# Agent attention and two feed-forward layers: the first batch's softmax over keys with its maximum in two halves, values among the scores

## The chip, the cores and the metric

The kernel runs on one core of one Trainium2 chip. The metric is device time in microseconds (us), from three runs of the same program, and the profile is one further execution of it. A NeuronCore has a matrix engine (TensorE, PE in the profile; its loads of stationary operands are a row of their own, PEld), a vector engine (VectorE, DVE), a scalar engine (ScalarE, ACT), GpSimd (POOL) and SyncE (SP), which here starts the transfers from memory. The engines run side by side, each takes its own instructions in order, and they wait for each other through semaphores. TensorE's clock has two levels, 1.2 and 2.4 GHz; the profile tells which share of full speed was granted in a stretch.

## The reference

```python
def _attn_ref(q, k, v, agents):               # q, k, v: (2, 12480, 128), agents: (2, 49, 128)
    scale = 1.0 / np.sqrt(q.shape[-1])
    def sm(a, b):
        s = scale * (a @ b.transpose(0, 2, 1))
        s = s - s.max(-1, keepdims=True)
        e = np.exp(s)
        return e / (e.sum(-1, keepdims=True) + 1e-09)
    a2k = sm(agents, k)
    agent_v = a2k @ v
    return (sm(q, agents) @ agent_v).astype(np.float32)
# x = that, as (24960, 128); w_in (128, 2048) and w_out (2048, 128) of each layer
h = x @ w_in;  x = ((h * np.cos(h)) @ w_out).astype(np.float32)
h = np.maximum(x @ w_in2, 0.0);  out = (h * h @ w_out2).astype(np.float32)
```

The four weight matrices come as 64-bit floats, everything else as 32-bit floats.

## The kernel before

The work has three stretches.

**The prologue** (lines 405 to 507) handles the first batch's keys and values and has to end before the first block of queries can start. The keys come as 13 transfers of 960 keys (`k_load`), each worked on in two halves of 480. `k_scores` multiplies a half with the agents (four matmuls of 120 keys, each printed by the trace as two instructions, since the operands are 32-bit floats), copies the scores to `s_t` on ACT and keeps a running maximum `rm` on DVE. Although one batch is wanted here, its moving operand holds the agents of both batches: 98 columns (`both` is True, lines 284 to 288). After the last of the 26 halves the maximum is finished: `k_max` reduces `rm`, `k_max0` turns it on PE, `k_max1` takes the maximum over keys, `k_max2` spreads it to all partitions with a second small matmul. Then `k_shift` subtracts it and `exps` takes the exponential, in five parts (`parts`), and `v_mm` multiplies each of the 13 groups of 960 with their values into one PSUM bank, `pav` (8 matmuls, 16 instructions a group). `agent_v` divides, and a short chain (`agent_v1`, `agent_v2`, `m_fast`) makes the first columns of the matrix `ms` that the first layer needs.

While this runs, pieces of the weights are converted from 64-bit floats: there are 16 pieces of 512 columns, 0 to 3 for `w_in1`, 4 to 7 for `w_out1`, 8 to 11 for `w_in2`, 12 to 15 for `w_out2`. `scale` is one instruction on ACT and one on POOL, `stage` four on DVE, `high` one on ACT, `add` three matmuls on PE (from piece 4 on), `low` one on ACT. For pieces above 8 the `t` of the four stages lies in PSUM.

Tables say what is loaded and done after which half or group: `LOAD0`, `LOADK`, `LOADV` for transfers (k, v, w for a piece, q), `EVK`, `EVV` for the rest. Loads of keys and values share 7 buffers in rotation, so a transfer waits until the group that is 7 places ahead has been used.

**The fill**, the first 8 of 416 steps (`FILL`; 52 blocks of 480 queries, 8 steps each). A step `s` does `stage_a` (two 128-wide chunks of the first layer: `h1_chunk` on PE, the sine on ACT, the product `g` on DVE, its high half `gh`), `stage_b` of an earlier step (six matmuls into `px` with `gh` and the remainder `gl`), and after the fill `stage_c` and `stage_d` of the second layer as well. Small tasks are hung on steps with `at(step, slot, ...)`: the rest of the weight pieces (a loop over tuples: piece, step of its load, step `s0` of its `scale`; the stages come at `s0 + 1`, `high` at `s0 + 2`, `add` and `low` at `s0 + 4`), the columns of `ms`, the queries' softmax. When block 0's `px` is complete, in step 8's turn, ACT makes `xh` and DVE `xl` from it (lines 746 and 747), which `stage_c` of step 9 waits for.

**The steady stretch**, steps 9 to 415, in which the second batch's keys and values are worked in between.

All is under a manual schedule: each engine runs its instructions in the order in which the code issues them.

Of the kernel before, what the change touches and what calls it, by code (L numbers as in the profile page):

```python
# [34 lines left out]
def agent_attention_moe_kernel(ctx, tc, q, k, v, agents, w_in1, w_out1, w_in2, w_out2, out):  # L35
# [19 lines left out]
    NKV, NRAW = 7, 4  # L55
# [46 lines left out]
    class Weights:  # L102
# [20 lines left out]
        def stage(self, i):  # L123
# [3 lines left out]
            if i == 0:  # L127

                self.a = tmp(0, 4) if self.n == 2 * NWP else tmp(1, 4)

                self.t = pso.tile([128, 512], F32, name="t", tag="o")[:, :WP] if self.n > 2 * NWP else None
# [52 lines left out]

    def stages(ws):
        for i in range(Weights.STAGES):
            for w in ws:
                w.stage(i)
# [93 lines left out]
    def k_scores(b, n, kT, ps, both):  # L282

        w = B * A if both else A
        for j in range(J):
            o = ps[:TP, j * w:(j + 1) * w]
            rhs = agT.rearrange("p b a -> p (b a)") if both else agT[:, b, :]
            nc.tensor.matmul(o, kT[:, j * TP:(j + 1) * TP], rhs, start=True, stop=True)
        sv = ps[:TP, :J * w].rearrange("p (t a) -> p t a", a=w)[:, :, b * A if both else 0:][:, :, :A]
        sn = s_t[:, n * J:(n + 1) * J, :]  # L290
        nc.scalar.activation(sn, sv, AF.Copy)
        h = n % 2
        eng = nc.vector
        if n // 2 == 1:
            eng.tensor_tensor(rm[:, h], s_t[:, h * J:(h + 1) * J, :], sn, ALU.max)
        elif n > 1:
            eng.tensor_tensor(rm[:, h], rm[:, h], sn, ALU.max)
# [10 lines left out]

    def k_max1(pm):
        ma = ag.tile([A, 1], F32, name="ma")  # L310
        nc.vector.tensor_reduce(ma, pm[:A, :TP], axis=AX.X, op=ALU.max)
# [12 lines left out]
    cuts = [0] + [min(KCH * c, NT) for c in (1, 4, 7, 10)] + [NT]  # L324
    parts = [slice(a, b) for a, b in zip(cuts, cuts[1:]) if b > a]
# [5 lines left out]
    def k_exp(x):  # L331
        exps(s_t[:, parts[x], :])
# [55 lines left out]
    def out_copy(po):  # L388
# [6 lines left out]
    LOAD0 = "kkwwkkkkkww"  # L395
    LOADK = {1: "k", 3: "k", 5: "k", 7: "k", 9: "k", 11: "kqq", 13: "v", 15: "v", 17: "wv", 19: "wv", 21: "v",
             23: "wv", 25: "wv"}
    EVK = {3: ["y0"], 5: ["s0", "a0"], 11: ["t0", "y2"], 13: ["s2", "a2"]}
    LOADV = {0: "v", 1: "v", 2: "v", 3: "v", 4: "v", 5: "vw"}
    EVV = {0: ["k2", "y4", "k3", "q0", "s4"], 1: ["e0", "y6", "k4", "h4", "s6", "h6", "n0"], 8: ["z8", "u8"], 10: ["b8"]}  # L400
    EVK = {n: [(e[0], int(e[1:])) for e in x] for n, x in EVK.items()}
    EVV = {n: [(e[0], int(e[1:])) for e in x] for n, x in EVV.items()}
    with tc.manual_schedule():

        with ExitStack() as c1:
# [4 lines left out]
            kcs, qTs, vcs, ws = [], [], [], []  # L410

            def load_w():
                ws.append(Weights(len(ws), *((sp, "raw", NRAW) if 4 <= len(ws) < 8 else (ag, "ld", 4))))

            def load_kv():
                if len(kcs) < NKC:
                    kcs.append(k_load(0, len(kcs), sp, "kv", NKV))
                elif len(vcs) < NKC:
                    vcs.append(v_load(0, len(vcs), sp, "kv", NKV))

            def load_q():
                if len(qTs) < G0:
                    qTs.append(q_load(*blocks[len(qTs)], sp, G0))

            loads = {"k": load_kv, "v": load_kv, "w": load_w, "q": load_q}

            def load(what):
                for c in what:
                    loads[c]()

            def scale(m):
                for w in ws[m:m + 2]:
                    w.scale()

            def high(m):
                for w in ws[m:m + 2]:
                    w.high()

            def add(m):
                for w in ws[m:m + 2]:  # L440
                    w.add()

            def top(m):
                for w in ws[m:m + 2]:
                    w.top()

            def wtop(m):
                nc.vector.tensor_reduce(wmax[:, NWP:], wmax[:, :NWP], axis=AX.X, op=ALU.max)

            load(LOAD0)  # L450
            make_identity(nc, ident)
            nc.vector.tensor_copy(identr, ident)
            nc.vector.tensor_scalar(nidentr, ident, -1.0, None, ALU.mult)

            for n in range(2 * NKC):
                i, hf = divmod(n, 2)
                pool, tag = (ps1, "h1") if hf == 0 else (ps2, "h2")
                k_scores(0, n, kcs[i][:, hf * J * TP:(hf + 1) * J * TP], pool.tile([128, 512], F32, name="pks", tag=tag),
                         True)
                load(LOADK.get(n, ""))  # L460
                for f, m in EVK.get(n, ()):
                    {"y": scale, "s": lambda m: stages(ws[m:m + 2]), "a": add, "t": top}[f](m)
            mb = k_max2(k_max1(k_max0(k_max())))
            qs = []
            for n in range(G0):
                qs.append(Queries(q_products(blocks[n][0], qTs[n], ps1.tile([128, 512], F32, name="pq", tag="h1")),
                                  sg_of(n)))

            def k_part(x):
                k_shift(mb, parts[x])  # L470
                k_exp(x)

            def q_part(m):
                for x in qs:
                    x.scores()

            def q_exp(m):
                for x in qs:
                    exps(x.sg)

            k_part(0)
            k_part(1)
            top(2)
            wtop(0)
            pav = pso.tile([128, 512], F32, name="pav", tag="o")
            pts = {}

            def first_p(m):
                pts[0] = q_finish(xs[0])
                sines()  # L490

            for i in range(NKC):
                v_mm(pav, vcs[i], i, i == 0, i == NKC - 1)
                load(LOADV.get(i, ""))
                for f, m in EVV.get(i, ()):
                    {"y": scale, "s": lambda m: stages(ws[m:m + 2]), "h": high,
                     "z": lambda m: ws[m].scale(), "u": lambda m: stages(ws[m:m + 1]), "b": lambda m: ws[m].high(),
                     "k": k_part, "q": q_part, "e": q_exp,
                     "n": lambda m: qs[0].normalize(xs[0])}[f](m)
            av = agent_v(pav[:A, :C + 1])  # L500
            first_p(0)
# [29 lines left out]
        for n, s_load, s0 in ((5, None, -4), (6, None, -3), (7, None, -2), (8, None, -1), (9, -3, 0), (12, -3, 1), (13, -3, 2),  # L531
                              (10, -1, 3), (14, 2, 4), (11, 3, 5), (15, 4, 6)):
# [373 lines left out]
```

## Time and profile before

| what | us |
|---|---|
| median of three runs | 2214.27 (2213.15 to 2214.34) |
| the profiled execution: its own time, its span | 2214.8, 2213.0 |
| busy in the span: PE, DVE, ACT, POOL | 2188.5, 1936.4, 1516.6, 1280.7 |
| first scores matmul, last one done | 5.00, 30.15 |
| first values matmul, last one done | 36.24, 61.41 |
| first matmul of step 0 | 64.70 |
| first matmul of step 9 | 108.05 |

The span runs from the first to the last instruction; the profiled execution's own time is 1.8 us more, and it lies 0.5 us above the median. PE is busy for 99% of the span, but a busy PE is not a PE at its peak: instructions overlap, and the clock is not told by the busy time. DMA engines are busy in the first 60 us and little after that.

### The profile page before, as it was taken

To read this page: it belongs to the slowest core of one execution; us is meant where nothing else is said; L and a number is where in the kernel's file an instruction comes from. 1 tells how busy PE (TensorE), PEld (TensorE's weight loads), DVE (VectorE), ACT (ScalarE), POOL (GpSimd) and SP (SyncE) were. 2 spreads that over 40 slices of the span, in tenths; PEclk is the share of its full clock that TensorE was granted. 3 is DMA by queue.
4 is the path that set the end of the run, shared out by engine and by line. 5 is a ranking of instruction groups with operands and counts; after the bars stand their busy time and mean duration, and the time that the engine had idled before them with its cause. 6 is when DMAs were issued, how large, how long until landed. Compare 5 with 4: busy or idle time off the path is not lost.

```text
span 2213.0 us, 30063 instructions
## 1 busy us (share of the span) xinstructions
PE 2188.5 (99%) x10593; PEld 1876.3 (85%) x10593; DVE 1936.4 (88%) x2431; ACT 1516.6 (69%) x2453; POOL 1280.7 (58%) x1285
## 2 busy tenths in 40 slices
PE   8999999999999999999999999999999999999998
PEld 8688888888888888888888888888888888888886
DVE  7788888888899999999988888888988988888897
ACT  4666766667767767767667767767776776776764
POOL 1455555556556556656556656566566565655664
PEclk9999999999999999999999999999999999999999
DMA  9200010000010010010000000000000000000000
GB/s 343 87 27 19 28 45 28 19 19 18 19 36 19 19 36 19 19 42 22 10 17 11 10 19 10 11 17 10 19 10 10 19 10 19 10 9 15 5 10 11
DMA packets 24952, 62.08 MB, mean 28 GB/s; under 512 B 2883, under 2 KB 16195, under 8 KB 24795
## 3 DMA queue, kind: packets, MB, share of 16 engines
q1 hardware_dynamic: 24795, 60.10, 8.5%
q8 instruction: 85, 1.39, 0.3%
q14 instruction: 72, 0.59, 0.1%
HBM read 47.31 MB, written 12.78 MB: 27 GB/s over the span
## 4 chain that ended last, share of the span: by engine, by line
PE 90%; DVE 7%; issue 1%; ACT 1%; DMA 0%; POOL 0%; SPq 0%; POOLq 0%; ACTq 0%; DVEq 0%
PE po L386 8%; PE ph L379 8%; PE po L384 8%; PE px L384 8%; PE ph L386 8%; PE ph L385 8%; PE ph L384 8%; PE px L386 7%; PE po L385 7%; PE ph L380 7%; PE px L385 7%; DVE g L713 2%; DVE sl L782 2%; PE misc L198 2%; PE pav L336 1%
## 5 line engine op out<-in xcount | busy, mean ns | idle before, releaser
L717 POOL TENSOR_SCALAR gh<-g 128x480 fp32r<-128x480 f32 x824 | 796.1, 984 | 671.6 <-DVE g L713 528.8
L757 ACT ACTIVATE r<-ph 128x480 f32<-128x480 f32 x832 | 472.8, 572 | 518.2 <-PE ph L386 487.1
L731 DVE TENSOR_TENSOR gl<-g,gh 128x960 fp32r<-128x960 f32 x409 | 587.0, 1435 | 84.4 <-POOL gh L717 84.3
L776 POOL TENSOR_SCALAR sh<-r 128x960 fp32r<-128x960 f32 (+1 forms) x425 | 464.5, 1093 | 203.6 <-issue 135.2
L713 DVE TENSOR_TENSOR g<-ph,g 128x480 f32<-128x480 f32 x832 | 504.8, 647 | 61.7 <-ACT g L703 61.7
L782 DVE TENSOR_TENSOR sl<-r,sh 128x960 fp32r<-128x960 f32 (+1 forms) x425 | 540.5, 1272 | 4.4 <-POOL sh L776 4.4
L703 ACT ACTIVATE g<-ph 128x480 f32<-128x480 f32 x832 | 429.0, 568 | 100.5 <-PE ph L380 61.2
L765 ACT ACTIVATE r<-r 128x960 f32<-128x960 f32 x407 | 410.8, 1009 | 12.9
L384 PE MATMUL px<-gh,wo 128*128 128x480 f32 x832 | 324.5, 390 | 0.0
L386 PE MATMUL po<-sl,wo 128*128 128x480 f32 x832 | 318.7, 383 | 2.6 <-DVE sl L782 2.2
L379 PE MATMUL ph<-pt,ms 98*128 98x480 f32 x832 | 320.6, 385 | 0.3 <-ACT ms L369 0.2
L384 PE MATMUL po<-sh,wo 128*128 128x480 f32 x832 | 318.4, 383 | 1.7 <-DVE ob L390 1.7
L386 PE MATMUL px<-gl,wo 128*128 128x480 f32 x832 | 316.9, 381 | 2.6 <-DVE gl L731 1.3
L386 PE MATMUL ph<-xl,wi 128*128 128x480 f32 x832 | 316.5, 380 | 1.2 <-DVE xl L747 1.2
L385 PE MATMUL ph<-xh,wi 128*128 128x480 f32 x832 | 317.4, 381 | 0.0
L384 PE MATMUL ph<-xh,wi 128*128 128x480 f32 x832 | 316.8, 381 | 0.0
L385 PE MATMUL px<-gh,wo 128*128 128x480 f32 x832 | 316.4, 380 | 0.0
L380 PE MATMUL ph<-pt,ms 98*128 98x480 f32 x832 | 315.4, 379 | 0.4 <-DVE ms L370 0.3
L385 PE MATMUL po<-sh,wo 128*128 128x480 f32 x832 | 315.3, 379 | 0.0
L386 PEld LDWEIGHTS po<-sl,wo 128*128 128x128 f32 x832 | 156.2, 188 | 37.5 <-DVE sl L782 11.7
L386 PEld LDWEIGHTS px<-gl,wo 128*128 128x128 f32 x832 | 156.3, 188 | 32.5 <-DVE gl L731 4.3
L386 PEld LDWEIGHTS ph<-xl,wi 128*128 128x128 f32 x832 | 156.4, 188 | 28.1 <-DVE xl L747 2.4
(132 smaller groups left out, 2323.1 us busy)
## 6 DMA issues: line engine op xcount, KB each, us to landing
kv<-in_k_dram SPq DMA_DIRECT2D x26, 480.0 KB, 5.3
qT<-in_q_dram SPq DMA_DIRECT2D x52, 240.0 KB, 3.9
out_dram<-ob SPq DMA_DIRECT2D x52, 240.0 KB, 2.1
kv<-in_v_dram SPq DMA_DIRECT2D x13, 516.0 KB, 8.6
kv<-in_v_dram SPq DMA_DIRECT2D x13, 483.8 KB, 4.7
raw<-in_w_in_dram SPq DMA_DIRECT2D x8, 512.0 KB, 6.4
raw<-in_w_out_dram SPq DMA_DIRECT2D x8, 512.0 KB, 8.8
agr<-in_agents_dram SPq DMA_DIRECT2D x1, 49.0 KB, 1.9
```

The source lines that it names most:

```text
L379: nc.tensor.matmul(ph[:, :T], ms[0][:, cs], p, start=True, stop=False)
L380: nc.tensor.matmul(ph[:, :T], ms[1][:, cs], p, start=False, stop=True)
L384: nc.tensor.matmul(ps[:, :T], w[0][:, cs], hi, start=first, stop=False)
L385: nc.tensor.matmul(ps[:, :T], w[1][:, cs], hi, start=False, stop=False)
L386: nc.tensor.matmul(ps[:, :T], w[0][:, cs], lo, start=False, stop=last)
L703: nc.scalar.activation(g[:, u, :], ph[:, :T], AF.Sin, bias=HALF_PI)
L713: nc.vector.tensor_tensor(g[:, u, :], phs[u][:, :T], g[:, u, :], ALU.mult)
L717: nc.gpsimd.tensor_scalar(gh[:, u, :], g[:, u, :], 1.0, 1.0, ALU.mult, ALU.mult)
L731: nc.vector.tensor_tensor(gl, g, gh.bitcast(F32), ALU.subtract)
L757: nc.scalar.activation(r[:, u, :], ph[:, :T], AF.Relu)
L776: nc.gpsimd.tensor_scalar(sh[:, u, :], r[:, u, :], 1.0, 1.0, ALU.mult, ALU.mult)
L782: nc.vector.tensor_tensor(sl[:, u, :], r[:, u, :], sh[:, u, :].bitcast(F32), ALU.subtract)
```

## The change

Code of the weight pieces, of the scores and of the prologue's order changes; the steps' arithmetic does not.

- `both` goes: the scores' moving operand is the 49 columns of one batch.
- The running maximum is kept in two parts, for the halves 0 to 13 and 14 to 25 (`NA` = 7 groups). The first part's maximum is finished among the scores, and the values of groups 0 to 6 use it, in one PSUM bank; groups 7 to 12 use the maximum of both, in a second bank. At the end the first sums are scaled with the exponential of the difference of the two maxima (`decay`, `first_sums`) and added.
- The tables become one string, `SCRIPT`: `k3` is half 3's scores, `v3` group 3's values, `R`, `T`, `P`, `M` the four parts of the maximum, `S` a part of shift and exponential, `z`, `u`, `a`, `h`, `t` scale, stages, add, high and maximum of a weight piece, `L...` loads.
- Keys and values share 9 buffers instead of 7, and two buffers instead of four hold raw pieces of `w_out1`.
- The prologue converts pieces 0 to 5 and only scales piece 6. Pieces 6, 7, 8, 12, 9, 13, 10, 14, 11, 15 have their stages in steps 0 to 9, one a step, `high` a step later, `add` and `low` three steps later. Before, steps 1 to 7 had the stages of 9, 12, 13, 10, 14, 11, 15, and the adds of 5 to 8 were in steps 0 to 3 and those of the seven in steps 4 to 10; now the adds of 5 are in step 0 and those of the ten in steps 3 to 12.

```diff
-    NKV, NRAW = 7, 4
+    NKV, NRAW = 9, 2
...
-    def k_scores(b, n, kT, ps, both):
-
-        w = B * A if both else A
+    def k_scores(b, n, kT, ps, n0=0):
+
         for j in range(J):
...
+            nc.tensor.matmul(ps[:TP, j * A:(j + 1) * A], kT[:, j * TP:(j + 1) * TP], agT[:, b, :], start=True, stop=True)
...
-        if n // 2 == 1:
-            eng.tensor_tensor(rm[:, h], s_t[:, h * J:(h + 1) * J, :], sn, ALU.max)
...
+        if (n - n0) // 2 == 1:
+            nc.vector.tensor_tensor(rm[:, h], s_t[:, (n - 2) * J:(n - 1) * J, :], sn, ALU.max)
...
+    NA = (NKC + 1) // 2
+    cuts = [0, 1, 3, 5, NA, NA + 1, NA + 3, NKC]
...
+    LATE = NWP + 2
+    WORDER = [0, 1, 2, 3, 4, 5, 6, 7, 8, 12]
...
+    SCRIPT = """Lkkwwkkkkkkk k0 k1 Lk k2 k3 z0 z1 Lv k4 k5 u0 a0 u1 a1 Lk k6 k7 Lv k8 k9 Lwk k10 k11 Lvw k12 k13 R0 t0 Lk k14 k15
+        Lv k16 k17 T0 P0 t1 Lqqv k18 k19 M0 S0 S1 Lwv k20 k21 z2 v0 Lvv S2 k22 k23 v1 Lwvv S3 u2 a2 k24 k25 z3 v2 Lvv R1 T1 P1
+        u3 a3 v3 Lvwwww M1 S4 S5 D1 v4 Q0 S6 q0 e0 v5 z4 z5 v6 F0 u4 h4 v7 u5 h5 v8 t2 t3 W0 v9 n0 v10 z6 v11 v12"""
...
+            pav = [p.tile([128, 512], F32, name="pav", tag=t) for p, t in ((pso, "o"), (psx, "x"))]
...
+            def values(i):
+                v_mm(pav[i >= NA], vcs[i], i, i in (0, NA), i in (NA - 1, NKC - 1))
...
+            def peak(h):
+
+                ma = mx["ma", h] = k_peak(mx["p"], f"ma{h}")
+                if h:
+                    nc.vector.tensor_tensor(ma, ma, mx["ma", 0], ALU.max)
+                mx["mw"] = k_wide(ma)
...
+            def decay(h):
+
+                d = mx["d"] = sp.tile([A, 1], F32, name="d")
+                nc.vector.tensor_tensor(d, mx["ma", 0], mx["ma", 1], ALU.subtract)
+                exps(d)
+
+            def first_sums(h):
+                acc = mx["acc"] = sp.tile([A, C + 1], F32, name="acc0")
+                nc.scalar.activation(acc, pav[0][:A, :C + 1], AF.Copy, scale=mx["d"])
...
+            nc.vector.tensor_tensor(acc, pav[1][:A, :C + 1], acc, ALU.add)
...
+        at(0, 1, lambda: ws[NWP + 1].add())
+        at(0, 1, lambda: ws[NWP + 1].low())
+        for s0, n in enumerate((6, 7, 8, 12, 9, 13, 10, 14, 11, 15)):
...
+            if s0:
+                at(s0 - 1, 1, each("scale"))
+            for m in range(Weights.STAGES):
+                at(s0, 1, each("stage", m))
+            at(s0 + 1, 1, each("high"))
+            at(s0 + 3, 1, each("add"))
+            at(s0 + 3, 1, each("low"))
```

On PE, the prologue before ran all scores (`pks`, 104 matmuls of 98 columns), the two small matmuls of the maximum (`misc<-ident`), the query products (`pq`) and then all values (`pav`):

```order
L288 MATMUL pks<-agT,kv 120x98 x104
L306 MATMUL misc<-ident,r_397 49x120
L318 MATMUL misc<-ident,mw 120x49
L198 MATMUL pq<-agT,qT 120x49 x8
L336 MATMUL pav<-kv,s 49x129 x104
```

Now it begins so:

```order
L279 MATMUL pks<-agT,kv 120x49 x72
L295 MATMUL misc<-ident,r_273 49x120
L279 MATMUL pks<-agT,kv 120x49 x8
L313 MATMUL misc<-ident,mw 120x49
L279 MATMUL pks<-agT,kv 120x49 x8
L332 MATMUL pav<-kv,s 49x129 x8
L279 MATMUL pks<-agT,kv 120x49 x8
L332 MATMUL pav<-kv,s 49x129 x8
L279 MATMUL pks<-agT,kv 120x49 x8
L332 MATMUL pav<-kv,s 49x129 x8
L295 MATMUL misc<-ident,r_441 49x120
L332 MATMUL pav<-kv,s 49x129 x8
```

The first values follow 88 score matmuls (22 halves) instead of 104, the last four halves lie between the groups of values, and every score matmul has 49 columns.

On DVE, steps 0 and 1 of the fill before (`g` is the product of `stage_a`, `ms` a piece of the first layer's matrix, `t` the stages of a weight piece):

```order
L370 SCALAR_TENSOR_TENSOR ms_102<-misc,safe,ms_101 98x256
L713 TENSOR_TENSOR g<-ph_666,g 128x480
L713 TENSOR_TENSOR g<-ph_670,g 128x480
L370 SCALAR_TENSOR_TENSOR ms_102<-misc,safe,ms_101 98x256
L713 TENSOR_TENSOR g<-ph_692,g 128x480
L713 TENSOR_TENSOR g<-ph_696,g 128x480
L370 SCALAR_TENSOR_TENSOR ms_102<-misc,safe,ms_101 98x512
```

and now:

```order
L366 SCALAR_TENSOR_TENSOR ms_102<-misc,safe,ms_101 98x256
L705 TENSOR_TENSOR g<-ph_658,g 128x480
L705 TENSOR_TENSOR g<-ph_662,g 128x480
L366 SCALAR_TENSOR_TENSOR ms_102<-misc,safe,ms_101 98x256
L134 TENSOR_SCALAR t<-t_591 128x512
L136 SCALAR_TENSOR_TENSOR t_679<-t_591,t 128x512
L139 TENSOR_SCALAR t<-t_679 128x512
L144 SCALAR_TENSOR_TENSOR wo_1_96<-raw,t 128x512
L705 TENSOR_TENSOR g<-ph_690,g 128x480
L705 TENSOR_TENSOR g<-ph_694,g 128x480
L366 SCALAR_TENSOR_TENSOR ms_102<-misc,safe,ms_101 98x512
```

Four stage instructions (piece 6) now stand ahead of step 1's `g`.

On DVE, step 8 before, from the remainder `gl` of step 7 on (`xl` is the remainder of block 0's result, which the second layer's first matmuls wait for; `sm` belongs to the queries):

```order
L731 TENSOR_TENSOR gl<-g,gh 128x960
L713 TENSOR_TENSOR g<-ph_999,g 128x480
L713 TENSOR_TENSOR g<-ph_1003,g 128x480
L747 TENSOR_TENSOR xl<-px,xh 128x480
L731 TENSOR_TENSOR gl<-g,gh 128x960
L713 TENSOR_TENSOR g<-ph_1037,g 128x480
L713 TENSOR_TENSOR g<-ph_1041,g 128x480
L218 TENSOR_REDUCE sm<-sgr 120x4
```

and now:

```order
L723 TENSOR_TENSOR gl<-g,gh 128x960
L705 TENSOR_TENSOR g<-ph_997,g 128x480
L705 TENSOR_TENSOR g<-ph_1001,g 128x480
L134 TENSOR_SCALAR t<-t_986 128x512
L136 SCALAR_TENSOR_TENSOR t_1017<-t_986,t 128x512
L139 TENSOR_SCALAR t<-t_1017 128x512
L144 SCALAR_TENSOR_TENSOR wi_1_98<-raw,t 128x512
L739 TENSOR_TENSOR xl<-px,xh 128x480
L723 TENSOR_TENSOR gl<-g,gh 128x960
L705 TENSOR_TENSOR g<-ph_1044,g 128x480
L705 TENSOR_TENSOR g<-ph_1048,g 128x480
L134 TENSOR_SCALAR t<-t_1023 128x512
```

The stages of piece 11 stand ahead of `xl` and those of piece 15 behind the next step's `g`.

## Rows read from the trace of the kernel before

**Rows 1.** The page: shares of the chain that ended last.
```profile
PE 90%; DVE 7%; issue 1%; ACT 1%; DMA 0%; POOL 0%; SPq 0%; POOLq 0%; ACTq 0%; DVEq 0%
```

**Rows 2.** Stretches: length, each engine's busy time, granted clock, DMA share, GB/s.
```profile
64.70:108.05 43.35, 39.50 (x148) 26.42 (x149) 36.22 (x62) 32.37 (x59) 25.91 (x30) 0.96 0.19 60
108.05:160.00 51.95, 51.95 (x244) 43.70 (x243) 42.84 (x59) 35.28 (x58) 30.06 (x32) 1.00 0.04 10
```

**Rows 3.** Timeline of PE in the prologue: start, length (us), instructions.
```profile
5.00 16.13 PE L288 MATMUL pks<-agT,kv 128*120 128x98 f32 x128 [5.00 <-DMA kv<-in_k_dram]
21.54 8.61 PE L288 MATMUL pks<-agT,kv 128*120 128x98 f32 x80 [0.41 <-ACT s L291]
...
33.13 3.18 PE L198 MATMUL pq<-agT,qT 128*120 128x49 f32 x16
36.24 25.17 PE L336 MATMUL pav<-kv,s 120*49 120x129 f32 x208
...
64.70 0.49 PE L379 MATMUL ph<-pt,ms 98*128 98x480 f32 x1
```

**Rows 4.** Timeline of PE's weight loads: runs of one kind, in narrow stretches.
```profile
4.97 4.65 PEld L288 LDWEIGHTS pks<-agT,kv 128*120 128x120 f32 x23 [4.97 <-issue]
21.51 8.47 PEld L288 LDWEIGHTS pks<-agT,kv 128*120 128x120 f32 x80 [0.54 <-ACT s L291]
33.83 2.32 PEld L198 LDWEIGHTS pq<-agT,qT 128*120 128x120 f32 x11
36.24 4.10 PEld L336 LDWEIGHTS pav<-kv,s 120*49 120x49 f32 x20
41.98 18.94 PEld L336 LDWEIGHTS pav<-kv,s 120*49 120x49 f32 x171
156.18 1.03 PEld L288 LDWEIGHTS misc<-agT,kv 128*120 128x120 f32 x8
```

**Rows 5.** Short stretches, columns as in Rows 2: the granted clock around PE's pauses.
```profile
30.20:33.10 2.90, 0.58 (x3) 0.40 (x3) 1.66 (x4) 0.32 (x1) 0.00 (x0) 1.00 1.04 410
33.50:36.00 2.50, 2.50 (x15) 2.50 (x14) 2.50 (x4) 1.09 (x2) 0.00 (x0) 0.50 1.02 410
...
40.40:42.40 2.00, 2.00 (x20) 2.00 (x19) 2.00 (x5) 2.00 (x5) 0.72 (x2) 1.00 0.74 227
78.60:80.60 2.00, 0.00 (x1) 0.00 (x0) 1.90 (x7) 0.56 (x2) 1.63 (x2) 1.00 0.03 4
```

**Rows 6.** Two stretches of the prologue, columns as in Rows 2: the transfers.
```profile
20.00:38.00 18.00, 15.22 (x119) 14.55 (x119) 16.16 (x38) 5.74 (x14) 1.09 (x2) 0.87 1.03 409
38.00:54.00 16.00, 16.00 (x136) 15.91 (x135) 14.21 (x29) 8.31 (x13) 2.69 (x4) 0.93 0.81 266
```

**Rows 7.** Timeline of DVE in steps 0 to 2; in brackets the idle time before.
```profile
68.09 0.48 DVE L370 SCALAR_TENSOR_TENSOR ms<-misc,safe,ms 98x256 fp32r<-98x256 f32 x1 [0.47 <-ACT ms L369]
69.76 1.22 DVE L713 TENSOR_TENSOR g<-ph,g 128x480 f32<-128x480 f32 x2 [1.18 <-ACT g L703]
...
72.33 0.68 DVE L135 TENSOR_SCALAR t<-t 128x512 int32<-128x512 int32 x1
...
74.50 0.69 DVE L145 SCALAR_TENSOR_TENSOR wi<-raw,t 128x512 fp32r<-128x512 uint16 x1
```

**Rows 8.** Timeline of DVE at the end of the fill.
```profile
108.87 0.66 DVE L747 TENSOR_TENSOR xl<-px,xh 128x480 fp32r<-128x480 f32 x1 [0.71 <-ACT xh L746]
...
112.52 1.93 DVE L731 TENSOR_TENSOR gl<-g,gh 128x960 fp32r<-128x960 f32 x1 [0.54 <-POOL gh L717]
```

**Rows 9.** Timeline of PE at the end of the fill, and in steps 9 and 10.
```profile
109.58 0.49 PE L386 MATMUL ph<-xl,wi 128*128 128x480 f32 x1
...
115.37 1.02 PE L161 MATMUL misc<-t,ident 128*128 128x512 f32 x2
...
116.70 0.38 PE L384 MATMUL px<-gh,wo 128*128 128x480 f32 x1
...
117.14 0.38 PE L386 MATMUL px<-gl,wo 128*128 128x480 f32 x1
```

More of the change, by code (lines that the diff above doesn't have):

```diff
@@ L409, in agent_attention_moe_kernel, with scores @@
             nc.scalar.activation(agT, agr, AF.Copy, scale=SCALE)
[L410 to L425, printed above, removed]
+            kcs, qTs, vcs, ws, mx, qs, pts = [], [], [], {}, {}, [], {}
             def load(what):
                 for c in what:
[L429 to L455, printed above, removed]
+                    if c == "k":
+                        kcs.append(k_load(0, len(kcs), sp, "kv", NKV))
+                    elif c == "v":
+                        vcs.append(v_load(0, len(vcs), sp, "kv", NKV))
+                    elif c == "q":
+                        qTs.append(q_load(*blocks[len(qTs)], sp, G0))
+                    else:
+                        n = WORDER[len(ws)]
+                        ws[n] = Weights(n, *((sp, "raw", NRAW) if NWP <= n < LATE else (ag, "ld", 4)))
+            pav = [p.tile([128, 512], F32, name="pav", tag=t) for p, t in ((pso, "o"), (psx, "x"))]
+            def scores(n):
                 i, hf = divmod(n, 2)
@@ L469, in k_part @@
[L469 to L488, printed above, removed]
+                         2 * NA if n >= 2 * NA else 0)
@@ L489, in first_p, with products, stages @@
+            def products(m):
+                for n in range(G0):
+                    qs.append(Queries(q_products(blocks[n][0], qTs[n], ps1.tile([128, 512], F32, name="pq", tag="h1")),
+                                      sg_of(n)))
+            def stages(n):
+                for i in range(Weights.STAGES):
+                    ws[n].stage(i)
+            def first_p():
                 pts[0] = q_finish(xs[0])
                 sines()
[L492 to L499, printed above, removed]
@@ L500, in agent_attention_moe_kernel @@
-            av = agent_v(pav[:A, :C + 1])
-            first_p(0)
+            do = {"k": scores, "v": values, "R": row_max, "T": turn, "P": peak, "M": to_all, "S": part, "D": decay, "F": first_sums,
+                  "Q": products, "q": lambda m: [x.scores() for x in qs], "e": lambda m: [exps(x.sg) for x in qs],
+                  "n": lambda m: qs[0].normalize(xs[0]), "z": lambda n: ws[n].scale(), "u": stages,
+                  "a": lambda n: ws[n].add(), "h": lambda n: ws[n].high(), "t": lambda n: ws[n].top(),
+                  "W": lambda m: nc.vector.tensor_reduce(wmax[:, NWP:], wmax[:, :NWP], axis=AX.X, op=ALU.max)}
```

88 lines of the change are left out of this document (38 added, 50 removed).

## The prediction

> **What bounds the kernel now.** I first read the page's chain of work that ended last: 90% of it is PE [rows 1], so a change counts only where it makes PE finish sooner or later. Then the table by stretches: from 108.05 us on PE has no idle time at all (51.95 of 51.95 us), while from 64.70 to 108.05 it is idle for 43.35 − 39.50 = 3.85 us and DVE is busy for 36.22 [rows 2]. So the fill, steps 0 to 8, is held up mostly by DVE, and what comes behind it by PE alone. The change touches only what lies ahead of step 13. All 400 steps behind it do the same work, so the time moves by what the prologue's end and the fill move.
>
> The timeline of PE gives the prologue [rows 3]. Scores run from 5.00 to 21.54 + 8.61 = 30.15, values from 36.24 to 61.41, and step 0 starts at 64.70. Between scores and values lie 6.09 us, in which the maximum is finished on DVE and PE does only the query products (3.18) and two small matmuls.
>
> The weight loads then show at what pace PE goes in each run [rows 4], since every instruction of these runs has a load of its own. With 98 columns: 80 loads in 8.47 us, 0.105 apart, and in the first run 23 in 4.65, 0.2 apart. With 49 columns: 11 in 2.32, 0.2 apart, and 8 in 1.03 much later, which holds one pause, so again 0.105. With 129 columns (values): 20 in 4.10, 0.21 apart, and 171 in 18.94, 0.11 apart. Two things follow. Each run has a slow and a fast pace with a factor of two between them, and 49 columns go no faster than 98 at either: what is paid is the load of 120 keys.
>
> Which pace holds is the granted clock [rows 5]. PE pauses from 30.20 to 33.10 (busy for 0.58 of 2.90), and from 33.50 to 36.00 the clock stands at 0.50, the 1.2 GHz level. In that stretch PE is busy for 2.50 of 2.50 us, all of it with query products of 49 columns, and the clock does not rise, neither within it nor at its end: the first 20 value loads still go 0.21 apart. By 40.40 it is 1.00 again, the 2.4 GHz level. At the kernel's start, 4.65 us of scores with 98 columns were enough to leave the slow pace.
>
> **The change part by part.**
>
> *Scores with 49 columns.* At equal clock this saves nothing (0.105 against 0.105 apart). But it takes away the columns with which the clock rose at the start. The only run of 49-column matmuls that began at the low level, back to back for 2.5 us, did not lift it [rows 5], and in the new order PE has nothing else for 22 halves but two small matmuls. I take the 0.2 pace for all of these: 22 halves of 8 instructions are 176 × 0.2 = 35.2 us, plus 0.4 for the two small matmuls, so the first values start at 5.0 + 35.6 = 40.6. The other bound is the pace of before, the first rival.
>
> The Trainium skill, page "TensorE: Matmul & The Clock Gate", section "Why this matters for your kernels", asks only that TensorE be kept continuously busy to reach full clock, and says nothing of how wide the matmuls are; the row of 33.50 to 36.00 speaks against taking "busy" for enough. By that rule the sum would be the first rival's, 2214; by the row it is 2230.
>
> *Values among the scores, two maxima.* The 6.09 us between scores and values go. Finishing the first maximum costs a reduction, two small DVE instructions and two small matmuls, while PE has six halves of scores (9.6 us at the slow pace) to run; the second lies beside the values. Nothing waits for either. What is left for PE behind 40.6, at full clock: 4 halves × 8 × 0.105 = 3.4, 208 value instructions × 0.11 = 22.9, 16 query products × 0.105 = 1.7, two small matmuls 0.4; together 28.4. The clock first has to come up: in before 4.10 us of values went at 0.21 instead of 0.11, a loss of 2.0, and I take that. Values end at 40.6 + 28.4 + 2.0 = 71.0. The new addition on DVE ahead of the division is small (129 columns; `xl`, 480 columns, takes 0.66 [rows 8]): 0.3. The prologue ends 71.3 − 61.4 = 9.9 us later than before.
>
> *Buffers, transfers.* In before the DMA engines moved 409 GB/s without a gap until 38 us, then 266, held back by buffers [rows 6], and the values never waited for them. At the slow pace PE uses a group of keys every 3.2 us instead of every 1.7, with two buffers more, so loads come earlier relative to their use: 0. If the scores went fast, buffers would come free earlier: the 16 × 266 = 4.3 MB moved from 38 to 54 us take 10.4 us at 409, so all but the last groups would be in by about 49 us, with the last values at 54.
>
> *DVE and ACT in the prologue* lose the stages of pieces 6 to 8 there. PE sets the end there, so that brings 0.
>
> *The fill.* The same number of stages as before stands in each of steps 1 to 7; what is added is one set in step 0, one in step 8, one in step 9. A set is four instructions from 72.33 to 74.50 + 0.69, 2.86 us [rows 7]. In step 0 it stands between `ms` (ends 68.57) and step 1's `g` (69.76), where DVE is idle for 1.18: `g` comes 1.7 later. Behind it wait ACT's `gh` and the next `ms`, and for these PE's next first-layer matmuls. In the steps that follow DVE has hardly an idle moment to take that back: +1.7. In step 8 the set stands ahead of `xl`, where DVE is idle for 0.71 [rows 8]; PE uses `xl` at once, 109.58 against 109.53 [rows 9], with the second layer's matmuls queued behind: 2.86 − 0.71 = +2.15. In step 9 the set delays `gl`, which before was done at 114.45 and needed by PE at 117.14 [rows 8, 9]: 2.7 of slack for 2.86, so 0 for the likely case and 2.9 at most, if the lateness of step 8 has used it up.
>
> *Adds.* Net, two adds move out of steps 1 and 2, where PE waits for others, into steps 11 and 12, where it never does. One add holds PE from 115.37 to 116.70, 1.33 [rows 9]: +2.7. What leaves steps 1 and 2 brings 0 to 2.7. I take 0, since PE sits idle a step later from 78.60 to 80.60 with DVE busy for 1.90 of that [rows 5].
>
> Fill together: 1.7 + 2.15 + 2.7 = 6.5, between 2 (the fill's idle 3.85 and the freed adds take up the rest) and 9.4.
>
> **Sum.** 9.9 + 6.5 = +16.4. The profiled execution took 2214.8, so 2231.2; it lay 0.5 above the median, so 2230.7, say 2230.
>
> **The rivals.**
>
> *1. The clock rises in the scores as before.* Then 23 loads take 4.65, the other 153 of the first 22 halves 16.1, and values begin at 5.0 + 4.65 + 16.1 + 0.4 = 26.1. With 28.4 and 0.3 the prologue ends at 54.8, 6.6 earlier. With the fill's 6.5 that is 2214: not slower. It turns faster (by over 0.2%, 4.4 us, which is about what a measurement of this kernel can tell from no change) where the fill costs less than 2.2. For it: the runs of 98 and 49 columns look the same in busy time. Against it: the stretch from 33.50, and it needs a second thing as well, that 49 columns hold the clock once it is up. 2208 to 2219.
>
> *2. The clock stays low in the alternation too.* Groups of values and halves of scores alternate until group 2; if only the unbroken run of values from there on lifts the clock, some 16 us go at the low level (three groups of 3.4, four halves of 1.6) and 8 are lost instead of 2: 2236. For it: here 4 us of unbroken values were needed. Against it: more than half of the time in the alternation is values.
>
> *3. The clock rises midway in the scores,* at a place that no row shows: 2219 to 2224.
>
> *4. The step 9 set is paid in full:* 2.9 more in the forecast, 2233; inside its range.
>
> **How the numbers follow.** Forecast, scores slow until the values begin: 0.75, own range 2224 to 2235 (the fill's bounds and 2 us for the clock). Rival 2: 0.08, 2232 to 2239. Rival 3: 0.04. Rival 1: 0.13, of which 0.04 beyond −0.2% and 0.09 within. The range from 2217 to 2238 leaves out most of rival 1 and the far end of rival 2, not quite 0.2. Slower by over 0.2% (above 2218.7): 0.87; within: 0.09; faster: 0.04.
>
> **What would show it.** Right: score loads 0.2 apart from 5 to 40 us and a first clock record of 1.0 only behind the first values; values ending near 71; step 0 near 74.5; step 9 some 12 us later than 108.05; `xl` behind four stage instructions. Wrong: scores 0.105 apart before the first values (rival 1), a PE that waits for transfers in the prologue, or a fill no longer than before. The forecast falls with the clock in the first 40 us, since that one term is worth 16.5 of its 16.4.

## The result and the profile after

The changed kernel takes 2238.84 us (median of four runs, 2236.45 to 2242.57), the one before 2214.31 on the same chip: a ratio of 1.0113, 95% interval 1.0095 to 1.0130. It is slower, by 24.5 us where 16 were forecast, and the time lies 0.8 above the upper end of the range. The profiled execution took 2240.73 with a span of 2238.9, so 25.9 of both is what the trace has to explain.

The page says little by itself: PE's share of the span is 99% in both kernels, and its share of the chain that ended last is 89% where it was 90% [rows 1].

```profile
PE 2211.4 (99%) x10596; PEld 1897.6 (85%) x10596; DVE 1924.2 (86%) x2438; ACT 1514.8 (68%) x2457; POOL 1285.8 (57%) x1285
...
PE 89%; DVE 8%; ACT 2%; issue 1%; DMA 0%; POOL 0%; SPq 0%; ACTq 0%; DVEq 0%; POOLq 0%
```

The timeline of PE in the prologue (start, time from the first start to the last end, what, how many) answers to [rows 3]:

```profile
5.12 29.00 PE L279 MATMUL pks<-agT,kv 128*120 128x49 f32 x144 [5.12 <-DMA kv<-in_k_dram]
...
37.91 3.43 PE L279 MATMUL pks<-agT,kv 128*120 128x49 f32 x16
41.27 3.68 PE L332 MATMUL pav<-kv,s 120*49 120x129 f32 x16
44.88 3.44 PE L279 MATMUL pks<-agT,kv 128*120 128x49 f32 x16
48.24 3.68 PE L332 MATMUL pav<-kv,s 120*49 120x129 f32 x16
51.85 3.44 PE L279 MATMUL pks<-agT,kv 128*120 128x49 f32 x16
55.22 3.68 PE L332 MATMUL pav<-kv,s 120*49 120x129 f32 x16
58.82 0.44 PE L295 MATMUL misc<-ident,r 120*49 120x120 f32 x1
59.19 2.23 PE L332 MATMUL pav<-kv,s 120*49 120x129 f32 x16
...
61.68 1.97 PE L332 MATMUL pav<-kv,s 120*49 120x129 f32 x16
63.59 1.88 PE L192 MATMUL pq<-agT,qT 128*120 128x49 f32 x16
65.39 14.37 PE L332 MATMUL pav<-kv,s 120*49 120x129 f32 x128
...
83.38 0.48 PE L375 MATMUL ph<-pt,ms 98*128 98x480 f32 x1
```

The same work is done twice here, at two paces. A group of values takes 3.68 three times, then 2.23, then 1.97; sixteen instructions with 49 columns take 3.44 in the scores and 1.88 in the query products. The change from one to the other lies near 59 us, and nothing is waited for in between. The low level lasted from the start to there: the first record of the clock in this trace is its rise, at 59.75 us. (In the stretches below, the clock's column says 1.00 ahead of that too, since it knows the level only from the first record on. The pace has to be read from the instructions.)

Stretches: scores and alternation (time, then busy time of PE, PEld, DVE, ACT and POOL, clock, DMA share, GB/s), and steps 0 to 8, which answer to [rows 2, 6]:

```profile
5.00:41.27 36.27, 36.15 (x180) 35.91 (x180) 15.44 (x35) 9.38 (x25) 1.19 (x2) 1.00 0.89 328
41.27:59.70 18.43, 18.43 (x85) 16.58 (x85) 7.70 (x16) 4.50 (x9) 1.73 (x2) 1.00 0.53 173
...
83.38:128.45 45.07, 37.59 (x140) 25.05 (x141) 38.66 (x66) 32.46 (x60) 27.40 (x31) 0.96 0.30 93
```

PE is busy without a gap in the scores and in the alternation, and transfers are not in the way: the DMA engines are busy for 0.89 and 0.53 of the time. Steps 0 to 8 take 45.07 where they took 43.35.

Behind the fill's last stages, `xl` is late as forecast. DVE and then PE around it [rows 8, 9]:

```profile
128.46 0.68 DVE L134 TENSOR_SCALAR t<-t 128x512 int32<-128x512 int32 x1
...
130.70 0.69 DVE L144 SCALAR_TENSOR_TENSOR wi<-raw,t 128x512 fp32r<-128x512 uint16 x1
131.31 0.65 DVE L739 TENSOR_TENSOR xl<-px,xh 128x480 fp32r<-128x480 f32 x1
```

```profile
132.01 0.49 PE L382 MATMUL ph<-xl,wi 128*128 128x480 f32 x1 [2.04 <-DVE xl L739]
```

Where the 25.9 us came from, by the first matmul of a step in both traces: step 0 starts 83.38 − 64.70 = 18.68 later; from there to the start of step 9 it takes 1.72 longer (45.07 − 43.35), from step 9 to step 13 another 4.72, of which 2.04 are the wait for `xl` and 1.34 each the adds in steps 11 and 12; steps 13 to 415 take 0.91 longer, what is behind them 0.11 less. So the fill is, in sum, where the forecast had it (6.44 against 6.5), and the prologue is not (18.68 against 9.9).

### The profile page after: what moved, and what is told of

It is laid out like the page before. It is cut to its first block, busy times and chain, and to the rows that moved or that the text cites. A ratio compares the mean times of both kernels' runs of the same rounds, so it can differ in the third digit from the quotient of the medians.

```text
span 2238.9 us, 30081 instructions
## 1 busy us (share of the span) xinstructions
PE 2211.4 (99%) x10596; PEld 1897.6 (85%) x10596; DVE 1924.2 (86%) x2438; ACT 1514.8 (68%) x2457; POOL 1285.8 (57%) x1285
## 4 chain that ended last, share of the span: by engine, by line
PE 89%; DVE 8%; ACT 2%; issue 1%; DMA 0%; POOL 0%; SPq 0%; ACTq 0%; DVEq 0%; POOLq 0%
PE po L382 8%; PE ph L382 8%; PE po L380 7%; PE ph L380 7%; PE po L381 7%; PE px L380 7%; PE ph L375 7%; PE ph L381 7%; PE px L382 7%; PE ph L376 7%; PE px L381 7%; PE pks L279 2%; DVE g L705 2%; DVE sl L774 2%; PE misc L192 1%; PE pav L332 1%
## 5 line engine op out<-in xcount | busy, mean ns | idle before, releaser
L723 DVE TENSOR_TENSOR gl<-g,gh 128x960 fp32r<-128x960 f32 x409 | 573.8, 1403 | 81.6 <-POOL gh L709 81.5
L768 POOL TENSOR_SCALAR sh<-r 128x960 fp32r<-128x960 f32 (+1 forms) x425 | 470.8, 1108 | 228.6 <-issue 156.1
```

The costliest lines, as they stand in the source:

```text
L723: nc.vector.tensor_tensor(gl, g, gh.bitcast(F32), ALU.subtract)
L768: nc.gpsimd.tensor_scalar(sh[:, u, :], r[:, u, :], 1.0, 1.0, ALU.mult, ALU.mult)
```

## The experiments

Two theories of the prologue. **Clock**: the change is slow because PE runs its narrow scores at the low level, and with other columns the same order is fast. **Order**: the values among the scores, with two maxima and scores in between, are slow by themselves. Then the fill is tried apart from the prologue, and last a version that uses what was learnt. "Fill" is the time from step 0's first matmul to step 13's, against that of before.

### Columns and clock

**1. The new order with 98 columns.**

```diff
-            nc.tensor.matmul(ps[:TP, j * A:(j + 1) * A], kT[:, j * TP:(j + 1) * TP], agT[:, b, :], start=True, stop=True)
+            rhs = agT.rearrange("p b a -> p (b a)") if both else agT[:, b, :]
+            nc.tensor.matmul(ps[:TP, j * w:(j + 1) * w], kT[:, j * TP:(j + 1) * TP], rhs, start=True, stop=True)
...
-                         2 * NA if n >= 2 * NA else 0)
+                         2 * NA if n >= 2 * NA else 0, True)
```

> The changed kernel with the scores' moving operand back at 98 columns, nothing else. Clock theory: the clock rises at about 10 us, score loads go 0.105 apart, values begin at 26 to 27 and end at 54 to 56, and with the longer fill (+6.4, as measured in the changed kernel) the time is 2214, between 2210 and 2219, some 25 below the changed kernel. Rival (the order itself costs: values among the scores, two maxima, loads in another sequence): the time stays above 2228.

Measured 2220.23, ratio 1.0022 (1.0013 to 1.0032): 18.6 less than the changed kernel, from operands twice as wide. The timeline of its PE:

```profile
5.30 18.08 PE L281 MATMUL pks<-agT,kv 128*120 128x98 f32 x144 [5.30 <-DMA kv<-in_k_dram]
...
27.65 1.97 PE L335 MATMUL pav<-kv,s 120*49 120x129 f32 x16
29.55 1.92 PE L281 MATMUL pks<-agT,kv 128*120 128x98 f32 x16
...
38.15 0.30 PE L298 MATMUL misc<-ident,r 120*49 120x120 f32 x1 [1.02 <-DVE r L293]
```

144 instructions take 18.08 where the 49-column ones took 29.00. The clock was up at 11.08 and stayed up to 72.5, so the first theory holds. But step 0 starts only 2.4 us before that of before (62.31), not 6.6, and the time came out above the range: even at full clock the order gains little, and the fill's 6.4 are more than that.

**2. The old order with 49 columns.** The call of `k_scores` gets `False` for `both`; nothing else differs from before.

> The kernel before with 49 columns in the scores, nothing else. Clock theory: 208 score instructions 0.2 apart, 41.6 us instead of 25.15, so values begin at 52 to 53 instead of 36.24, all behind it unchanged: 2231, between 2228 and 2233. Rival (the order costs, not the columns): 2214.

Measured 2232.06, ratio 1.0078 (1.0061 to 1.0095). Step 0 starts 16.95 later, and behind it nothing changes.

```profile
5.02 41.81 PE L288 MATMUL pks<-agT,kv 128*120 128x49 f32 x208 [5.02 <-DMA kv<-in_k_dram]
...
53.53 24.82 PE L336 MATMUL pav<-kv,s 120*49 120x129 f32 x208
```

208 narrow instructions in 41.81 us, 0.2 apart to the last, and the clock rises at 56.87, after 3.3 us of unbroken values. This one word costs more than two thirds of what the whole change does.

**3. 98 columns in the last six halves alone** (20 to 25, the last two ahead of the first values and the four in the alternation): experiment 1's edit, with `both` true for `n >= 20`.

> The changed kernel with 98 columns in the last six halves only (20 to 25, the two ahead of the first values and the four among the values), 49 in the first twenty. If it is the 49-column halves that keep the clock low among the values: the clock rises 4 to 6 us behind half 20, at 42 to 45 instead of 59.8, values end 7 to 8 earlier, 2231, between 2228 and 2235. Rival (the change between two kinds of matmuls, or the small matmuls, keep it low, whatever the width): 2236 to 2243.

Measured 2234.04, ratio 1.0091 (1.0074 to 1.0108).

```profile
37.91 3.51 PE L281 MATMUL pks<-agT,kv 128*120 128x98 f32 x16
41.35 1.97 PE L335 MATMUL pav<-kv,s 120*49 120x129 f32 x16
...
72.17 0.56 PE L244 MATMUL misc<-identr,xs 120*98 120x120 f32 x4
```

The clock rises at 41.29, at the end of the first wide pair of halves, and the values end at 72.2 instead of 79.8, 1.2 from the forecast's 71.0. Step 0 starts 11.15 later than before (forecast 9.9). So the forecast's sum for this stretch (30.4 from first values to last; 30.8 here) comes out about right once the clock is up, but not by its parts: its 2.0 at the low level are not there, and paces that were rounded down and a wait of 0.85 stand in their place.

**4. The last four halves ahead of all values**, so that the values are unbroken; 49 columns stay.

```diff
-  k20 k21 z2 v0 Lvv S2 k22 k23 v1 Lwvv S3 u2 a2 k24 k25 z3 v2 Lvv R1
+  k20 k21 z2 k22 k23 k24 k25 v0 Lvv S2 v1 Lwvv S3 u2 a2 z3 v2 Lvv R1
```

> The changed kernel with the last four halves of scores ahead of the first group of values, so that the values run almost without a break. Clock theory: the clock rises some 4 us behind the first values, the loss at the low level there is 2 us instead of 9, values end at 74 to 75 instead of 79.8, time 2233, between 2230 and 2236. Rival (the values are late for another cause: loads, shift or exponential): no change, 2236 to 2243.

Measured 2237.92, ratio 1.0101 (1.0085 to 1.0118): no clear gain, and a miss by 2.

```profile
38.39 9.83 PE L279 MATMUL pks<-agT,kv 128*120 128x49 f32 x48
48.15 8.26 PE L332 MATMUL pav<-kv,s 120*49 120x129 f32 x48
```

The clock rose at 53.84, 5.7 us after the first values, and step 0 starts 2.9 us earlier than in the changed kernel. The mechanism is there, at about half of the 5 to 6 us expected, and the fill gave half of that back: it takes 1.4 longer than in the changed kernel. The clock fell three times in it, for 3.4 us each (91.39, 98.22, 128.94), once in the changed kernel.

**5. 98 columns in the first six halves alone** (`n < 6`).

> The changed kernel with 98 columns in the first six halves only, 49 in the other twenty. If 49 columns hold a clock that is up: as with 98 in all, 2220. If they do not: the clock falls behind half 6 and stays low to the values, two or three us below the changed kernel, 2235, between 2232 and 2240. I hold the second likelier, since the pause that dropped the clock in the fill also had PE at work for part of the time.

Measured 2224.23, ratio 1.0041 (1.0027 to 1.0054): a miss. The theory had the clock fall as soon as the wide halves are over. It rose at 10.86 and stayed up to 24.51, through 11.5 us of 49 columns (from 13.03 on), then fell and stayed low until 48.40. PE and clock in three stretches:

```profile
11.00:23.20 12.20, 12.17 (x117) 12.05 (x115) 10.10 (x24) 5.70 (x16) 1.19 (x2) 1.00 1.03 413
23.20:30.00 6.80, 6.72 (x37) 6.46 (x38) 4.63 (x12) 2.83 (x7) 0.00 (x0) 0.60 1.02 405
30.00:48.00 18.00, 18.00 (x83) 16.16 (x82) 7.52 (x14) 4.27 (x9) 1.74 (x2) 0.50 0.76 278
```

PE is busy for 6.72 of 6.80 us where the clock falls, and for all of the 18 us in which it doesn't come back. This trace is of the slowest of the five runs, 2229.86; the two fastest, 2222.07 and 2222.29, show a mean granted clock of 0.996 against its 0.993, so their low stretch was probably shorter. No profile shows it.

**6. 49 columns throughout, behind eighteen wide matmuls.** This asks whether 49 columns can run fast at all.

```diff
+                    early = psm.tile([128, 512], F32, name="early", tag="m")
+                    for j in range(18):
+                        nc.tensor.matmul(early[:, :128], ident, ident, start=True, stop=True)
```

> The changed kernel as it is, 49 columns in all scores, with eighteen 128 by 128 matmuls of the identity ahead of the first scores (36 instructions, at 0.2 each about 7 us from 1.4 on, so the scores begin near 8.5 instead of 5.1). They compute nothing that is used. Theory (narrow matmuls don't lift the clock, but keep it once it is up): clock up before the scores or in their first us, the scores 0.105 apart; if it stays up as in the kernel with six wide halves, until about 24, the rest goes like that kernel: values begin near 29, the low level holds through the alternation, and step 0 lies 7 to 9 us behind before, time 2224 to 2230. If nothing drops it, the prologue is that of the kernel with 98 columns and 3 us: step 0 near 65, time 2223. Rival (narrow matmuls let the clock fall as soon as the wide ones are gone): scores 0.2 apart from about 10 us on, values begin near 43, time 2236 to 2242.

Measured 2222.89, ratio 1.0053 (1.0033 to 1.0074), 16 us less than the changed kernel, of which this kernel holds every instruction.

```profile
1.37 6.48 PE L492 MATMUL early<-ident 128*128 128x128 f32 x36 [1.37 <-POOL ident masks.py:199]
7.68 15.22 PE L279 MATMUL pks<-agT,kv 128*120 128x49 f32 x144
...
27.25 3.24 PE L332 MATMUL pav<-kv,s 120*49 120x129 f32 x16
30.42 1.88 PE L279 MATMUL pks<-agT,kv 128*120 128x49 f32 x16
```

The same 144 instructions that took 29.00 take 15.22, 0.105 apart. The clock rose at 6.0, fell at 26.5, came back at 29.9 in the first group of values and stayed up through the narrow halves of the alternation. Step 0 starts at 62.96, 20.4 us earlier than in the changed kernel. The time is that of the theory's second case (2223), and step 0 lies 2 us ahead of it, though the clock does fall, for 3.4 us. The fill takes 1.6 longer than in the changed kernel, with a further fall of the clock at 111.81. It isn't safe: one run of the five took 2234.59, at a mean granted clock of 0.990 against 0.996 of the others. By an estimate from these, 0.006 of 2223 us at half the pace is 27 us more at the low level and 13 us lost, which is about its 12. No profile was taken of that run.

### The fill

**7. 98 columns and the old fill:** pieces 6 to 8 are converted in the prologue again, the steps hold the seven pieces as before. Of the edit, the line of the script is shown; the loop over the fill's pieces is that of before again.

```diff
-        u3 a3 v3 Lvwwww M1 S4 S5 D1 v4 Q0 S6 q0 e0 v5 z4 z5 v6 F0 u4 h4 v7 u5 h5 v8 t2 t3 W0 v9 n0 v10 z6 v11 v12"""
+        u3 a3 v3 Lvwwww M1 S4 S5 D1 v4 Q0 S6 q0 e0 v5 z4 z5 v6 F0 u4 h4 v7 u5 h5 z6 z7 v8 t2 t3 W0 u6 h6 v9 n0 u7 h7 z8 v10 u8 h8 v11 v12"""
...
```

> The changed kernel with 98 columns in the scores, pieces 6 to 8 converted in the prologue and the fill's tasks of the kernel before. Clock theory with the fill as forecast: prologue 5 to 7 shorter than in the kernel before, fill as in it, 2208, between 2206 and 2212, faster than both kernels. If the fill's 6.4 is not from the moved pieces: 2213 to 2215, as with 98 columns alone. Rival (the order itself costs): above 2214.

Measured 2219.85, ratio 1.0024 (1.0014 to 1.0033): a miss by 12, and no clear gain over experiment 1. The fill is that of before (−0.07), but step 0 starts 4.3 us later than before. The timeline of PE, then of DVE, shows why:

```profile
58.59 0.56 PE L244 MATMUL misc<-identr,xs 120*98 120x120 f32 x4
64.83 0.34 PE L348 MATMUL misc<-ident,av 49*128 49x49 f32 x1 [5.69 <-DVE av L343]
```

```profile
63.21 0.69 DVE L144 SCALAR_TENSOR_TENSOR wi<-raw,t 128x512 fp32r<-128x512 uint16 x1
63.82 0.28 DVE L494 TENSOR_TENSOR acc<-pav,acc 49x129 f32<-49x129 f32 x1
```

The values are done at 58.6, and DVE is still at the stages of pieces 6 to 8 until 63.8, ahead of the sum that the prologue ends with. Where they stand, the faster prologue has no room on DVE for them: the wait is 5.0 longer than the one of experiment 1 (0.64). And the clock falls in it, at 62.45: what lies between the wait and step 0 takes 4.18 instead of 2.48. The two are the 6.7 by which step 0 starts later than in experiment 1.

**8. The changed kernel (49 columns) with the old fill:** the same edit.

> The changed kernel with the fill's tasks of the kernel before and pieces 6 to 8 in the prologue, 49 columns kept. The moved pieces theory: steps 0 to 13 are 6.4 shorter, as with 98 columns; the slow prologue leaves DVE room, so step 0 starts as in the changed kernel: 2232, between 2229 and 2236. Rival (the fill's length comes from another part, or the prologue's DVE is late here too): 2236 or more.

Measured 2239.06, ratio 1.0104 (1.0089 to 1.0119): the same as the changed kernel, 3 above the range and as the rival had it.

```profile
86.03 0.34 PE L345 MATMUL misc<-ident,av 49*128 49x49 f32 x1 [5.01 <-DVE av L340]
```

Step 0 starts 25.5 later than before, and the fill is 0.24 longer. Here too the prologue pays what the fill gains, with this wait and a fall of the clock in it, at 84.91.

**9. Before with the ten-piece fill alone;** pieces 6 to 8 leave the prologue.

```diff
-        for n, s_load, s0 in ((5, None, -4), (6, None, -3), (7, None, -2), (8, None, -1), (9, -3, 0), (12, -3, 1), (13, -3, 2),
...
+        at(0, 1, lambda: ws[NWP + 1].add())
...
+        for s0, n in enumerate((6, 7, 8, 12, 9, 13, 10, 14, 11, 15)):
```

> The kernel before with the changed fill alone: pieces 6 to 8 out of the prologue, ten pieces in steps 0 to 9. The moved pieces theory: step 0 starts as before (PE sets the prologue's end), steps 0 to 13 take 6.4 more: 2221, between 2219 and 2223. Rival (the prologue gains what the fill loses): 2214.

Measured 2222.74, ratio 1.0035 (1.0022 to 1.0048): inside the range, by other parts. Step 0 starts 1.6 earlier (the clock was low for 3.4 us between scores and values, for 6.8 in before), and the fill is 7.9 longer. The waits for `xl` (2.0) and the two adds (1.32 and 1.33) are there, and the clock falls at 112.94 for 3.4 us.

**10. 98 columns, and no stages in step 8:** pieces 11 and 15 a step later.

```diff
-        for s0, n in enumerate((6, 7, 8, 12, 9, 13, 10, 14, 11, 15)):
+        for s0, n in zip((0, 1, 2, 3, 4, 5, 6, 7, 9, 10), (6, 7, 8, 12, 9, 13, 10, 14, 11, 15)):
```

> With 98 columns in all halves, the stages of pieces 11 and 15 moved from steps 8 and 9 to steps 9 and 10, their adds from 11 and 12 to 12 and 13. If the set ahead of the remainder of block 0's result is what makes PE wait: that wait of 2 us goes, the two adds cost 2.7 as before, 2218.5, between 2217 and 2219.5. Rival (the lateness only moves to the next steps): 2220.

Measured 2222.07, ratio 1.0029 (1.0018 to 1.0041): above the range, and 2 above the rival's 2220 too. The wait for `xl` is gone, but in experiment 1's trace it was only 0.5 (the clock there was low from 106.65 to 110.06), not the changed kernel's 2.0. Another has come, in this row of PE's waits (time in total, how often, the longest):

```profile
PE po L383 <- DVE sm L215: 2.4, 1, 2.4
```

So the lateness moved, as the rival said: DVE's work doesn't shrink by being moved within the fill.

### A version that keeps the clock

**11. Before, with the clock kept up between scores and values:** two further halves of scores with 98 columns while the maximum is finished, and query products with 98 columns.

```diff
+            for n in range(2):
+                pool, tag = (ps1, "h1") if n == 0 else (ps2, "h2")
+                px0 = pool.tile([128, 512], F32, name="pks", tag=tag)
+                for j in range(J):
+                    nc.tensor.matmul(px0[:TP, j * B * A:(j + 1) * B * A], kcs[-1][:, (n * J + j) * TP:(n * J + j + 1) * TP],
+                                     agT.rearrange("p b a -> p (b a)"), start=True, stop=True)
...
```

> The kernel before with PE kept at work while the maximum is finished: two more halves of scores with 98 columns behind the last one, into PSUM that nothing reads, and the query products with 98 columns. Clock theory: no low stretch between 33.4 and 40.3, products 0.105 apart, values from the start 0.11 apart, values end 3 to 4 us earlier, 2211, between 2209 and 2212.5, below both kernels. Rival (the clock falls with the wait itself or counts time, not the width): as before or later, 2214 to 2217.

Measured 2213.23 against 2214.94, ratio 0.9993 (0.9984 to 1.0002), 0.7 above the range. The clock is up from 9.49 to 77.76 without a low stretch (before it fell at 33.45 and came back at 40.28):

```profile
32.82 1.92 PE L200 MATMUL pq<-agT,qT 128*120 128x98 f32 x16
34.67 23.23 PE L338 MATMUL pav<-kv,s 120*49 120x129 f32 x208
```

The query products take 1.92 instead of 3.18 with twice the columns, the values 23.23 instead of 25.2, and step 0 starts 3.5 earlier. Of that the span keeps 3.3 (2209.7) and the median 1.7; between span and own time lie 2.6 us in this execution and 1.8 in before, which is 0.8 of the difference. The interval holds "no change".

**12. The same, with the clock lifted ahead of the scores** by nine wide matmuls, as in experiment 6.

> Before with the clock kept up between scores and values (the kernel with two dummy halves and wide query products), and nine 128 by 128 matmuls of the identity, some 3.7 us from 1.4 on, ahead of the first scores; neither dummy computes anything that is used. Theory (the chain through the prologue is PE at its clock): the first 4.5 us of scores go at full pace instead of half, 2 us less than without these nine: step 0 5 to 5.5 us earlier than before, time 2211 (2209 to 2213), the shortest of all. Rival: the scores then wait for the transfers of keys, which set the pace at the start, and nothing is gained: 2213, with idle time of PE ended by kv. Second rival: the nine end later than the first keys arrive, 5.0, and the scores start later by as much as they gain: 2213.

Measured 2212.26 against 2214.24, ratio 0.9990 (0.9981 to 0.9999): the shortest median of all, inside the range of the theory, but not by its mechanism.

```profile
1.37 4.21 PE L458 MATMUL early<-ident 128*128 128x128 f32 x18 [1.37 <-POOL ident masks.py:199]
5.37 3.93 PE L290 MATMUL pks<-agT,kv 128*120 128x98 f32 x32
10.47 8.61 PE L290 MATMUL pks<-agT,kv 128*120 128x98 f32 x80 [1.17 <-DMA kv<-in_k_dram]
20.31 10.29 PE L290 MATMUL pks<-agT,kv 128*120 128x98 f32 x96 [1.23 <-DMA kv<-in_k_dram]
```

The clock is up at 6.3, and PE then waits twice for keys, 2.4 us together, as the rival said. Step 0 starts 2.8 us earlier than before, not 5. Against experiment 11 nothing is gained that could be told apart; against before the interval just excludes "no change"; the gain is 0.1%.

## Why the prediction was wrong

- **Scores with 49 columns: right.** Forecast 0.2 apart and the first values at 40.6; measured 29.00 us for 144 and 41.27. Experiments 1 and 2 show that it was the columns: each kernel with narrow scores from the start on ran slow, in both orders, and 98 columns in the same order were fast. Rival 1 fell.
- **Values among the scores, nothing waits: right at the pace at which they ran.** No gap of PE in the alternation. In experiments 1 and 3, at full clock, PE waits for the second maximum for 1.02 and 0.85 us, which "nothing waits for either" had at none.
- **The step that failed** is the term "The clock first has to come up: in before 4.10 us of values went at 0.21 instead of 0.11, a loss of 2.0, and I take that". It carried the 2.0 from a run of unbroken values over to one in which narrow scores stand between the groups. Behind the first values the low level lasted from 41.27 to 59.75, 18.5 us. From first values to last, the changed kernel took 38.5 us (41.27 to 79.76), and experiment 3, in which the clock came up at 41.29, took 30.8 (41.35 to 72.2, with its wait of 0.85): so the low level cost 38.5 − (30.8 − 0.85) = 8.5 instead of 2. Of the 8.8 us by which the values ended later than forecast, 6.5 are this term, 0.7 the later start, and 1.6 paces that were rounded down (16 value instructions take 1.90 from start to start, not 16 × 0.11). This is rival 2 nearly word for word ("some 16 us go at the low level … and 8 are lost instead of 2: 2236"), which had got 0.08.
- **Why 0.08 was too little.** The argument against rival 2 was that more than half of the time in the alternation is values. It had no row behind it. The row it had, 4 us of unbroken values, was for the rival. Experiment 4 weighs the same from the other side: unbroken values lifted the clock after 5.7 us, broken ones after 18.5. And the rise came where rival 2 had put it, in the run of values behind the last scores: 4.5 us into it in the changed kernel (55.22 to 59.75), 4.8 in experiment 5 (43.62 to 48.40), 5.5 in experiment 8 (55.54 to 61.01).
- **The second thing that rival 1 was said to need,** "that 49 columns hold the clock once it is up", is true for 11.5 us in experiment 5 and 19 in experiment 6; then the clock fell in both, and in experiment 5 it stayed low into the values. So the doubt had something in it, but here the clock didn't rise in the scores at all, and that alone failed rival 1.
- **The fill: right in sum (6.44 for 6.5), partly by luck.** The wait for `xl` (2.04 for 2.15), the adds (2.68 for 2.7) and the set of step 9 (nothing) are as forecast. The 1.72 up to step 9 is not the single delay of 1.7 that the forecast carried on: step 2 starts 1.50 later (beyond the 18.68 of step 0), but step 4 no later at all (−0.10), and steps 4 and 5 bring 1.67 that no term names. The fall of the clock, which the sum didn't have, lies in step 2 in the changed kernel (93.89) and in step 3 in before (81.24). Experiment 9 shows the fill without the new prologue, at 7.9 with a second fall of the clock in it; in experiment 1 the same 6.44 has other parts (2.33 up to step 9, 0.5 of waiting for `xl`).
- **DVE in the prologue, "that brings 0": right for the forecast's order, but it had another side.** At the places tried in experiments 7 and 8 the stages couldn't have stayed in the prologue either: 5 to 5.7 us of waiting for DVE and 1.7 at the low level behind it, instead of 6.4 in the fill.
- **What stays open.** The kernels with the new order take 0.8 (experiment 8) to 1.4 us (experiment 1) more between steps 13 and 415, which do the same work (experiment 10, with an add in step 13, is left aside); those with the old order don't, experiment 9 with the new fill included (0.05). No run here explains it. Nor do the runs tell why unbroken values lifted the clock after 3.3 us in experiment 2 and after 5.7 in experiment 4, or what makes the clock fall in the fill of one kernel and not of another.

The Trainium skill, page "TensorE: Matmul & The Clock Gate", section "Why this matters for your kernels", asks for a TensorE that is kept continuously busy to reach full clock, and against drops for no idle gaps between bursts of matmuls. The traces here agree with neither as a sufficient condition: PE was busy for 36.15 of 36.27 us in the scores and for 18.43 of 18.43 behind them at the low level, and in experiment 5 the clock fell in a stretch with 6.72 of 6.80 busy.

The Trainium skill, page "Perfetto Trace Analysis", section "Identifying the Most-Contended Engine", calls the busy share of matmuls a poor measure of how near TensorE is to its peak. This case agrees: the page of the profile gives PE 99% in both kernels, 24.5 us apart, and PE is busy for 36.15 of 36.27 us in scores that went at half the pace.

## What to carry to other kernels

Columns that are computed for nothing can be worth their place: here 98 columns cost no more than 49 (0.105 apart at the full level and 0.2 at the low one, for both), and the extra ones were what lifted the clock. Before narrowing a matmul, or putting narrow ones between wide ones, find in the trace at which level such a run went and what lifted it, and don't carry the rise of an unbroken run over to a mixed one. Work that is taken off a prologue to shorten it is paid where it goes, if the engine that does it has no idle time there. And a sum that comes out right is no proof of its parts: look at where each part went.

## What the runs showed of the hardware

- The level depends on what came before, not only on what runs: the same 144 instructions of 49 columns took 29.00 us at the start of the changed kernel and 15.22 behind 6.5 us of matmuls of 128 columns (experiment 6). Narrow matmuls at the low level went on for 36 us (changed kernel) and 42 us (experiment 2) without lifting it, and at the full level for 11.5 us (experiment 5) and 19 (experiment 6) until it fell.
- The clock can fall while PE has almost no gap: at 24.51 in experiment 5 and at 26.5 in experiment 6, each within 2 us of one of the two small matmuls of the first maximum. That these are the cause wasn't tried.
- Runs of some of the programs with narrow scores spread more: 2236.45 to 2242.57 for the changed kernel, 2222.07 to 2229.86 in experiment 5 and 2222.64 to 2234.59 in experiment 6, against 2213.15 to 2214.91 for before beside the first, and 2211.85 to 2212.78 in experiment 12, whose clock is up from 6.3 to 77.9 us. That narrow scores are the reason isn't shown: experiment 2 has them throughout and spreads from 2231.46 to 2232.88.
